# Converting a weight piece in two parts, moving three loads to another queue, and narrowing what the operand sums wait for

## The chip, the cores and the metric

The kernel runs on one core of one Trainium2 chip. The metric is the device time of one execution in microseconds (us), median of the runs. Engines are named as the profile names them: PE (TensorE matmul), PEld (its weight loads), DVE (VectorE), ACT (ScalarE), POOL (GpSimd), SP (SyncE, which here only issues DMAs; the profile calls its queue SPq).

## The reference

Two blocks follow each other. The first is a linear recurrence over time, for 4 batches, 8 heads, 768 steps and 48 channels a head:

```python
f = 1.0 / (1.0 + np.exp(-f_logit))
for t in range(S):
    state = f[:, :, t, :, None] * state + np.einsum('bhd,bhe->bhde', k[:, :, t], v[:, :, t])
    y[:, :, t] = np.einsum('bhd,bhde->bhe', q[:, :, t], state)
```

Its output is reshaped to `x`, 3072 tokens by 384 features, and goes through a multiplicative feed-forward block:

```python
a = x @ w1            # 384 x 1024
b = x @ w2            # 384 x 1024
h = a * b @ w3        # 1024 x 1024
return h @ w_out      # 1024 x 384
```

The weights arrive as 64-bit floats. A core reads them as pairs of 32-bit words and makes 32-bit floats of them.

## The kernel before

**Recurrence.** The 3072 tokens are cut into 24 chunks of 128 (`u` in the code), six to a batch. For a chunk, four loads (f, k, q, v) land; ACT turns f into gates (L523); DVE runs a forward and a backward scan over them (L531, L553) and scales q and k by the results (L547, L561). PE turns K round (L600), forms the products of K and Q inside a chunk (L576 or L586, copied by ACT at L706 or L709, masked by POOL at L715), updates the state (L632 or L692) and forms the outputs (L614 and L620, or L660 and L679, called a visit below). For chunks 0 to 4 PE turns K (L600); from chunk 5 on ACT splits K into halves of words, a DMA transposes them (L735), and ACT puts them together (L740). The outputs of chunks 0 and 1 are brought into the layout of `x` by PE (L904); those of later chunks go through DRAM, written by SP (L896) and gathered by POOL (L899).

**Weights.** `fetch` loads a piece of a weight as raw word pairs into one of a few raw areas of the tile `place`, and converts it: ACT treats the low words (L1432), DVE shifts the high words (L1447, "shift"), combines sign and low words (L1451, "sign"), and adds the two (L1457, "join"). w1 and w2 are each cut into two halves of 512 columns, so there are four pieces of 128 x 1536 numbers, called A (w1, first half), B (w2, first half), C (w1, second half) and D (w2, second half). The order `EARLY = "23ACBD"` makes DVE do the scans of chunks 2 and 3, then A, C, B and D. The raw area of A is used again by D; the raw areas that follow hold four pieces of w_out and eight of w3, in turn over three places. A load into an area waits for whatever reader `users` lists for the piece before.

**Feed-forward.** `w3 @ w_out` is formed on the core once: eight folds of 16 matmuls (L1496) need all four w_out pieces and one w3 piece each, and ACT stores their results (L1503) as `wc`. Tokens go through in six blocks of four chunks. Block 0 uses the plain product: `part` issues, for each of eight column groups `jc`, one matmul group with w1 (copied by ACT, L965) and one with w2 (multiplied on DVE, L970). Such a group is six matmul records of line L928 in 128x256 form, and is called an up group below; there are 32 of them. Later blocks use seven or fewer products on sums of the operands, so DVE forms ten sums of w1 and w2 (L1529, `w12_sums`, written over raw areas that are no longer needed) and four sums of `wc` (L1543, `wc_sums`). `down` multiplies by `wc`; its matmuls m1, m2 and m3 read `wc` itself and m4 to m7 read sums of it.

**Order of the work.** All of it is entered as tasks in `Plan`, with an engine, a cost, dependences and a priority. `listed` runs through time, always takes the task that can start first (ties go by priority), and so writes one fixed order for each engine; on the chip each engine follows its order and waits on semaphores. Where the plan leaves PE idle for at least 0.43 us in its first 130 us, matmuls on a constant are put in (`idle`, L408), so busy time of L408 is time in which PE has no work. SP's order is such a list too: a DMA that waits for its raw area holds up the DMAs behind it. In `front`, the loads of v of chunks 0 to 3 go to SP and later ones to POOL (L515).

The lines that tie the turns of DVE together are these:

```python
for a, b in zip("1" + EARLY, EARLY):
    for t in first[b]:
        t["deps"] += last[a] if a != "1" else [tk[1]["q"], tk[1]["k"]]
```

Of the kernel before, what the change touches and what calls it, by code (L numbers as in the profile page):

```python
# [37 lines left out]
I32 = mybir.dt.int32  # L38
# [7 lines left out]
P = 128  # L46
C = 128
# [35 lines left out]
WITH_DMA = 1.2  # L83
# [215 lines left out]
def ranged(ctx, tc, q, k, f_logit, v, w1, w2, w3, w_out, out, ident, w12, wc, left):  # L299
# [182 lines left out]
    def front(u):  # L482
# [30 lines left out]
        def load_v():  # L513
            s["v"] = at(12288 + NQ, DM) if u == 3 else loads.tile([P, DM], F32, name="vt")
            (nc.sync if u < UB else nc.gpsimd).dma_start(s["v"], v[u])  # L515
# [3 lines left out]
            ask[3], **({} if u < UB else {"issue": WITH_DMA, "eng": "POOL"}),  # L519
# [277 lines left out]
    def rest(u):  # L797
# [117 lines left out]
        else:  # L915
            t["z"] = moves(2, 197, 300, written, [t["y"]], n0 - 100, 0.8)
# [16 lines left out]
    def ffn(n):  # L933
# [16 lines left out]
        def part(c0, c1, jcs):  # L950
# [22 lines left out]
            for jc in jcs:  # L973
# [3 lines left out]
                pa = plan.add("PE", cost, up(jc, 0), x + pieces[0, h], n0, takes=["f"])  # L977
                ka = takes_ab(jc, plan.add("ACT", 0.2 + nt * 0.28 / 384, keep_a(jc), [pa], -10, frees=[pa]))
                pb = plan.add("PE", cost, up(jc, 1), x + pieces[1, h] + [pa], n0 - 5, takes=["f"])
# [284 lines left out]
        def down(i):  # L1264
# [99 lines left out]
            got0, got1 = (s["done"][i] + wc_sums for i in range(2))  # L1364
# [7 lines left out]
            pe("m6", m6, [q["m1"], q["S1"]], -3 if n == NB - 1 else -1, takes=["f"])  # L1372
# [3 lines left out]
            pe("m7", m7, [q["u2"], q["S2"]], -3)  # L1376
            dve("u3", 0.36, u3, [q["m7"]] + old("c22"))
            pe("m5", m5, [q["S0"], q["m2"], q["m6"]] + [q["m7"]] * (n == NB - 1), -3, takes=["f"])
            dve("c22", 0.36, c22, [q["m5"], q["u3"]] + stores[-4:-2])
            pe("m4", m4, [q["u3"]], -4)  # L1380
# [29 lines left out]
    def fetch(loads_, where, prio, due, dst, waits=(), deps=()):  # L1410
# [33 lines left out]
        s = {}  # L1444

        def shifted():
            nc.vector.tensor_scalar(m.bitcast(U32), hi, 3, None, ALU.logical_shift_left)  # L1447

        def signed():
            s["to"] = dst()  # L1450
            nc.vector.scalar_tensor_tensor(  # L1451
                s["to"].bitcast(U32), hi, 0x80000000, lo, ALU.bitwise_and, ALU.bitwise_or
            )

        def joined():
            to = s["to"].bitcast(I32)
            nc.vector.tensor_tensor(to, m.bitcast(I32), to, ALU.add)  # L1457

        past = [joins[i] for i in mine if i in joins]
        h = plan.add("DVE", 0.16 + 0.27 * w, shifted, landed + past, due, shared=True)  # L1460
        g = plan.add("DVE", 0.16 + 0.53 * w, signed, [*low, h] + list(waits), due)
        j = plan.add("DVE", 0.16 + 0.53 * w, joined, [h, g], due - 1, shared=True)
        parts.append((g, j))
        joins.update({i: j for i in mine})
        got.append(g)
        return [j]

    def weights():
        due = dict(zip(((0, 0), (1, 0), (0, 1), (1, 1)), DUE))
        for item in (x for x in EARLY if x in "ABCD"):  # L1470
# [178 lines left out]
    first, last = {}, {}  # L1649
    for item in EARLY:  # L1650
        if item in "ABCD":
            half, which = divmod("ABCD".index(item), 2)
            mine = pieces[which, half]
            first[item], last[item] = [j["deps"][0] for j in mine], mine
        else:
            t = tk[int(item)]
            first[item], last[item] = [t["p"]], [t["q"], t["k"]]
# [389 lines left out]
```

## Time and profile before

| | |
|---|---|
| Time, median of 3 runs | 452.43 us (452.41 to 453.13) |
| The profiled execution: its time, its span | 452.64 us, 450.9 us |
| PE busy | 442.3 us, 98% of the span |
| DVE busy | 357.1 us, 79% |
| ACT busy | 253.6 us, 56% |
| POOL busy | 96.0 us, 21% |
| Granted TensorE clock, mean | 0.998 |

A time in the profile counts from the start of the span. Busy PE time includes the idle-filling matmuls of L408, and the ends of matmuls are modelled, so whether PE has work is read from the chain of waits, which gives the true spacing, and from the rows of L408. The span ends 1.74 us short of the execution's time (452.64 less 450.9).

### The profile page before, as it was taken

How to read it: one execution, taken by the hardware profiler on the slowest of the kernel's cores; microseconds unless marked ns; L12 is line 12 of the kernel's file. 1: busy time of each engine (PE TensorE's matmuls, PEld its weight loads, DVE VectorE, ACT ScalarE, POOL GpSimd, SP SyncE). 2: the span in 40 equal slices, each digit the busy share in tenths (PEclk: the TensorE clock that was granted, in tenths of full speed). 3: DMA queues.
4: the chain of work that ended last, by engine and by line, in shares of the span. 5: the costliest groups of instructions: out<-in, count | busy, mean ns of one | idle time of the engine just before them, and what ended most of it. 6: DMA issues, size and time to landing. Idle time of an engine off the chain costs nothing.

```text
span 450.9 us, 11720 instructions
## 1 busy us (share of the span) xinstructions
PE 442.3 (98%) x4720; PEld 386.2 (86%) x4720; DVE 357.1 (79%) x615; ACT 253.6 (56%) x559; POOL 96.0 (21%) x132
## 2 busy tenths in 40 slices
PE   7999999999999999999999999999999999999995
PEld 6788885566899888889988889998899988889995
DVE  8999998999898978998889958965669557667541
ACT  4576245554546768676676346656666656666100
POOL 9551003133432344344333102000020000000000
PEclk9999999999999999999999999999999999999999
DMA  6998699784566786677653156563264612331111
GB/s 177 265 401 252 251 319 318 206 201 125 127 146 173 204 184 161 141 176 194 168 145 87 27 160 218 175 206 100 93 197 154 213 47 93 94 94 48 36 71 39
DMA packets 51949, 73.10 MB, mean 162 GB/s; under 512 B 22849, under 2 KB 35010, under 8 KB 50866
## 3 DMA queue, kind: packets, MB, share of 16 engines
q1 hardware_dynamic: 49202, 64.05, 48.3%
q0 software_dynamic: 2688, 8.26, 6.4%
q8 instruction: 38, 0.62, 0.6%
q14 instruction: 21, 0.17, 0.1%
HBM read 58.88 MB, written 9.04 MB: 151 GB/s over the span
## 4 chain that ended last, share of the span: by engine, by line
PE 95%; DVE 1%; SPq 1%; DMA 1%; issue 0%; POOL 0%; POOLq 0%; DVEq 0%
PE f L928 29%; PE f L1024 17%; PE l L1179 13%; PE f L1179 10%; PE f L1496 9%; PE l L928 5%; PE py L660 3%; PE pa L586 2%; PE py L679 2%; PE pa L692 2%; SPq L497 1%; PE f L408 1%; DMA ab<-in_k_dram 1%; PE l L1024 1%; DVE K L561 0%
## 5 line engine op out<-in xcount | busy, mean ns | idle before, releaser
L715 POOL TENSOR_SCALAR_AFFINE_SELECT A<-A 64x512 f32<-64x512 f32 (+1 forms) x46 | 47.7, 1037 | 45.3 <-ACT A L709 43.1
L928 PE MATMUL f<-place 128*128 128x192 f32 x240 | 42.4, 327 | 0.0
L928 PE MATMUL f<-xt,w 128*128 128x256 f32 x192 | 42.3, 380 | 0.0
L1496 PE MATMUL f<-place 128*128 128x384 f32 x128 | 42.2, 489 | 0.0
L928 PEld LDWEIGHTS f<-xt,w 128*128 128x128 f32 x192 | 36.2, 190 | 4.9
L928 PEld LDWEIGHTS f<-place 128*128 128x128 f32 x240 | 39.6, 190 | 0.2
L1024 PE MATMUL f<-xt,w 128*128 128x256 f32 x156 | 39.2, 379 | 0.0
L1496 PEld LDWEIGHTS f<-place 128*128 128x128 f32 x128 | 24.1, 190 | 16.1
L899 POOL DMA_DIRECT2D xt<-yt x22 | 16.8, 765 | 96.9 <-PE l L1179 52.3
L1024 PEld LDWEIGHTS f<-xt,w 128*128 128x128 f32 x156 | 29.6, 190 | 4.0
L531 DVE TENSOR_TENSOR_SCAN fwd<-gate,floor 112x512 f32<-112x512 f32 x24 | 30.3, 1263 | 1.0 <-ACT gate L523 0.2
L553 DVE TENSOR_TENSOR_SCAN bwd<-gate,back 112x512 f32<-112x512 f32 x24 | 29.7, 1236 | 0.7
L740 ACT COPY kt<-halves 128x896 uint16<-128x896 uint16 x19 | 22.9, 1205 | 4.7 <-DMA halves<-A 4.7
L1024 PE MATMUL f<-place 128*128 128x256 f32 x92 | 24.9, 388 | 0.0
L1432 ACT ACTIVATE place<-place 128x512 f32<-128x512 uint32 (+2 forms) x24 | 21.3, 891 | 4.8 <-DMA place<-in_w_dram 2.7
L875 ACT ACTIVATE ys<-py 112x512 f32<-112x512 f32 x22 | 13.1, 596 | 19.1 <-PE py L679 19.1
L928 PE MATMUL f<-wc,ab 128*128 128x192 f32 x128 | 23.7, 329 | 0.1
L732 ACT COPY A<-K 112x1024 uint16<-112x1024 uint16 x19 | 19.8, 1042 | 3.8 <-DVE K L561 3.8
L928 PEld LDWEIGHTS f<-wc,ab 128*128 128x128 f32 x128 | 21.2, 190 | 0.7 <-PE f L408 0.5
L523 ACT ACTIVATE gate<-f 112x512 f32<-112x512 f32 x22 | 13.9, 633 | 12.6 <-DMA f<-in_f_logit_dram 7.8
L838 POOL TENSOR_TENSOR G<-lasts,gate 112x4 f32<-112x4 f32 x20 | 9.6, 479 | 52.3 <-ACT gate L523 26.8
L515 POOL DMA_DIRECT2D vt<-in_v_dram x20 | 11.5, 575 | 40.5 <-PE py L660 35.3
(292 smaller groups left out, 1061.8 us busy)
## 6 DMA issues: line engine op xcount, KB each, us to landing
place<-in_w_dram SPq DMA_DIRECT2D x21, 512.0 KB, 6.9
A<-in_w_dram SPq DMA_DIRECT2D x19, 512.0 KB, 3.8
place<-in_w_dram SPq DMA_DIRECT2D x8, 1024.0 KB, 6.6
q<-in_q_dram SPq DMA_DIRECT2D x46, 96.0 KB, 2.9
out_dram<-o SPq DMA_DIRECT2D x23, 192.0 KB, 2.7
k<-in_k_dram SPq DMA_DIRECT2D x44, 96.0 KB, 2.8
yt<-ys SPq DMA_DIRECT2D x44, 96.0 KB, 2.9
xt<-yt POOLq DMA_DIRECT2D x22, 192.0 KB, 4.1
```

The source lines that it names most:

```text
L523: nc.scalar.activation(gate[u % 2][:, 0:NQ], fu, AF.Sigmoid)
L531: nc.vector.tensor_tensor_scan(s["P"], gate[u % 2][:, 0:NQ], floor, 0.0, ALU.mult, ALU.max)
L553: nc.vector.tensor_tensor_scan(s["R"][:, ::-1], gate[u % 2][:, NQ:0:-1], back[:, ::-1], 0.0, ALU.mult, ALU.max)
L715: nc.gpsimd.affine_select(out=a, in_=a, pattern=pattern, compare_op=ALU.is_ge, fill=0.0, base=0, channel_multiplier=-1,)
L732: nc.scalar.copy(apart.rearrange("p (two n) -> p two n", two=2), s["K"].bitcast(U16).rearrange("p (n two) -> p two n", two=2))
L740: nc.scalar.copy(to, halves.rearrange("p (two n) -> p two n", two=2))
L899: nc.gpsimd.dma_start(block_xt()[:, :, cols], s["yt"].rearrange("(k p) c -> p k c", p=P))
L928: nc.tensor.matmul(out_, lhsT=lhs[i], rhs=rhs[i], start=start and i == 0, stop=i == len(lhs) - 1, skip_group_check=True,)
L1024: nc.tensor.matmul(q[nm][:, which * TH : which * TH + TH], lhsT=lhs[i](which), rhs=rhs[i], start=start and which == 0 and i == 0, stop=i = ...
L1179: nc.tensor.matmul(banks[g, c][:, which * TH : which * TH + TH], lhsT=lhs, rhs=x_node(a), start=first and which == 0, stop=True, skip_grou ...
L1432: nc.scalar.activation(part_.bitcast(F32), part_, AF.Copy, bias=2.0, scale=2.0**-51)
L1496: nc.tensor.matmul(w3s["p", jc], lhsT=w3s[jc][:, kc * P : kc * P + P], rhs=wos[:, kc], start=(kc == 0), stop=(kc == KF - 1),)
```

## The change

It has five parts. Piece A is converted in two parts of 256 columns a row block (`CUT`, `cuts`), A0 and A1, each with its own shift, sign and join; up groups wait for the part that they read. The v loads of chunks 0, 1 and 2 are issued by ACT's queue (`BY_ACT`). The ten sums of w1 and w2 wait for the converted pieces and for the raw areas that they overwrite, instead of for the last three converted pieces of all; m1, m2, m3 and the operand sums of `down` wait for `wc`, and only m4 to m7 also for its sums. Chunk 5 is turned on PE like chunks 0 to 4. Two of the plan's estimates move (the issue of a DMA by POOL 1.2 to 1.0, the way of y through DRAM 0.8 to 2.5), the raw areas of w_out and w3 are taken one place earlier in their turn, and an area is given free by the join instead of by the sign step.

```diff
-WITH_DMA = 1.2
+CUT = "A"
+TURNS = ('2', '3', 'A0', 'A1', 'C', 'B', 'D')
+BY_ACT = (0, 1, 2)
+WITH_DMA = 1.0
...
-            (nc.sync if u < UB else nc.gpsimd).dma_start(s["v"], v[u])
+            (nc.scalar if u in BY_ACT else nc.sync if u < UB else nc.gpsimd).dma_start(s["v"], v[u])
...
-            ask[3], **({} if u < UB else {"issue": WITH_DMA, "eng": "POOL"}),
+            ask[3], **({"eng": "ACT"} if u in BY_ACT else {} if u < UB else {"issue": WITH_DMA, "eng": "POOL"}),
...
-        if u > 4:
+        if u > 5:
             crossing(u)
...
-            t["z"] = moves(2, 197, 300, written, [t["y"]], n0 - 100, 0.8)
+            t["z"] = moves(2, 197, 300, written, [t["y"]], n0 - 100, 2.5)
...
-                pa = plan.add("PE", cost, up(jc, 0), x + pieces[0, h], n0, takes=["f"])
+                pa = plan.add("PE", cost, up(jc, 0), x + pieces[0, h][: jc % KH * len(pieces[0, h]) // KH + 1], n0, takes=["f"])
...
-            got0, got1 = (s["done"][i] + wc_sums for i in range(2))
+            got0, got1 = (s["done"][i] + folds for i in range(2))
...
-            pe("m6", m6, [q["m1"], q["S1"]], -3 if n == NB - 1 else -1, takes=["f"])
+            pe("m6", m6, [q["m1"], q["S1"]] + wc_sums, -3 if n == NB - 1 else -1, takes=["f"])
...
-        h = plan.add("DVE", 0.16 + 0.27 * w, shifted, landed + past, due, shared=True)
-        g = plan.add("DVE", 0.16 + 0.53 * w, signed, [*low, h] + list(waits), due)
-        j = plan.add("DVE", 0.16 + 0.53 * w, joined, [h, g], due - 1, shared=True)
-        parts.append((g, j))
+        past = [joins[i] for i in mine if i in joins]
+        ended = []
+        for c in range(cuts):
+            def of(t, c=c):
+                t = t.rearrange("p (k n) -> p k n", k=len(loads_))
+                return t[:, :, c * t.shape[2] // cuts : (c + 1) * t.shape[2] // cuts] if cuts > 1 else t
...
+            at_once = due + 0.1 * c
+            h = plan.add("DVE", 0.16 + 0.27 * w / cuts, shifted, landed + past, at_once, shared=True)
+            g = low if by_act else [plan.add("DVE", 0.16 + 0.53 * w / cuts, signed, [*low, h, *waits], at_once)]
+            j = plan.add("DVE", 0.16 + 0.53 * w / cuts, joined, [h, *g, *waits], at_once - 1, shared=True)
+            parts.append((h, j))
+            ended.append(j)
         joins.update({i: j for i in mine})
-        got.append(g)
-        return [j]
+        got += ended
+        return ended
...
+                cuts=2 if item in CUT else 1,
...
-                [(0, 2 * DM, src)], 2048 * ((13 + i // 2) % NRAW), 25 + 2.2 * i, 45 + 2.2 * i,
+                [(0, 2 * DM, src)], 2048 * ((12 + i // 2) % NRAW), 25 + 2.2 * i, 45 + 2.2 * i,
...
-                [(0, KF * P, src)], 2048 * ((17 + jc) % NRAW), 36 + 6 * jc, 50 + 6 * jc, w3_piece(jc),
+                [(0, KF * P, src)], 2048 * ((16 + jc) % NRAW), 36 + 6 * jc, 50 + 6 * jc, w3_piece(jc),
...
-        ready = [x for p in parts[-NRAW:] for x in p] + [x for p in pieces.values() for x in p]
+        whole = [x for p in pieces.values() for x in p]
         for which in range(2):
             for i in range(5):
-                w12_sums.append(plan.add("DVE", 0.69, sum_up(i, which), ready + w12_sums[-1:], 100 + i))
+                over_ = holders((which * 5 + i) * KH * P, KH * P)
+                w12_sums.append(plan.add("DVE", 0.69, sum_up(i, which), whole + over_ + w12_sums[-1:], 100 + i))
...
-    for a, b in zip("1" + EARLY, EARLY):
-        for t in first[b]:
-            t["deps"] += last[a] if a != "1" else [tk[1]["q"], tk[1]["k"]]
+    for (_, before), (t, _) in zip(chain, chain[1:]):
+        t["deps"] += before
```

The two other m lines of `down` that read sums (m7 and m5) and m4 get `wc_sums` in the same way as m6, and the up groups with w2 are narrowed like those with w1. `by_act` is false everywhere.

More of the change, by code (lines that the diff above doesn't have):

```diff
@@ L976, in part @@
                 n0 = 100 * n + 50 + 10 * (jc >= KH)
-                pa = plan.add("PE", cost, up(jc, 0), x + pieces[0, h], n0, takes=["f"])
+                pa = plan.add("PE", cost, up(jc, 0), x + pieces[0, h][: jc % KH * len(pieces[0, h]) // KH + 1], n0, takes=["f"])
                 ka = takes_ab(jc, plan.add("ACT", 0.2 + nt * 0.28 / 384, keep_a(jc), [pa], -10, frees=[pa]))
-                pb = plan.add("PE", cost, up(jc, 1), x + pieces[1, h] + [pa], n0 - 5, takes=["f"])
+                pb = plan.add("PE", cost, up(jc, 1), x + pieces[1, h][: jc % KH * len(pieces[1, h]) // KH + 1] + [pa], n0 - 5, takes=["f"])
                 kb = plan.add("DVE", 0.16 + nt * 0.4 / 384, times(jc), [pb, ka], -10, frees=[pb])
@@ L1443, in fetch @@
         mine = range(a0 // 512, (a0 + total + 511) // 512)
[L1444 to L1457, printed above, removed]
@@ L1648, in ranged @@
             ffn(u // UB)
[L1649 to L1654, printed above, removed]
+    chain = [(tk[1]["p"], [tk[1]["q"], tk[1]["k"]])]
+    for item in TURNS:
+        if item[0] in "ABCD":
+            half, which = divmod("ABCD".index(item[0]), 2)
+            js = pieces[which, half] if len(item) == 1 else [pieces[which, half][int(item[1])]]
+            chain.append((js[0]["deps"][0], js))
         else:
             t = tk[int(item)]
-            first[item], last[item] = [t["p"]], [t["q"], t["k"]]
-    for a, b in zip("1" + EARLY, EARLY):
-        for t in first[b]:
-            t["deps"] += last[a] if a != "1" else [tk[1]["q"], tk[1]["k"]]
+            chain.append((t["p"], [t["q"], t["k"]]))
+    for (_, before), (t, _) in zip(chain, chain[1:]):
+        t["deps"] += before
     ready_at = 0.0
```

18 lines of the change are left out of this document (14 added, 4 removed).

## The prediction

> **What bounds the kernel now.** I read the page for the shares, then the busy time by stage, then the rows of line L408 alone (matmuls on a constant: PE without work), and the chain of waits last, since only it gives the true spacing of matmuls. Columns of the stage rows: stretch, its length, busy time of PE, PEld, DVE, ACT and POOL with instructions, granted clock, DMA share, GB/s.
>
> ```profile
> 35.60:61.70 26.10, 26.10 (x126) 22.96 (x123) 23.90 (x31) 12.36 (x26) 1.94 (x4) 1.00 0.81 255
> 67.10:114.00 46.90, 46.90 (x441) 28.64 (x444) 44.30 (x56) 24.02 (x44) 13.91 (x13) 1.00 0.73 209
> 122.80:446.00 323.20, 323.10 (x3536) 296.06 (x3536) 244.25 (x467) 189.53 (x433) 55.41 (x76) 1.00 0.47 134
> ```
>
> PE has no hole from 35.60 us on, at full clock; in the last stretch 0.1 us of 323.2 is missing. DVE is next: 23.90 of 26.10 us and 44.30 of 46.90 us in the stages where weights are converted, so it has little room there. Where PE only seems busy, L408 tells (columns: stretch, its length, busy time of PE and of PEld in that line, clock, DMA):
>
> ```profile
> 10.00:20.00 10.00, 3.56 (x14) 2.50 (x14) 1.00 0.89 230
> 20.00:30.00 10.00, 2.23 (x10) 1.74 (x10) 1.00 1.03 399
> ```
>
> So spare PE time lies in the first 30 us, 3.56 and 2.23 us of it in these two stretches. The chain of waits (start, length, what; a record is one pass, and an up group is six of L928) places it:
>
> ```profile
> 25.06 1.73 PE f L408 x8
> 26.79 0.44 PE py L660 x12
> ...
> 28.72 0.46 issue
> ...
> 29.73 0.63 PE f L408 x2
> 30.36 3.89 PE f L928 x18
> ...
> 61.73 0.39 PE f L600 x4
> 62.11 5.20 PE f L928 x24
> 67.31 5.16 PE f L1496 x16
> ...
> 115.59 6.67 PE f L928 x30
> 122.26 0.45 PE f L408 x2
> ...
> 122.76 1.57 PE f L928 x8
> ...
> 444.96 1.31 PE f L928 x8
> ```
>
> The first up group starts at 30.36 us. From there to 446.27 (444.96 + 1.31) PE does real work but for 0.45 us at 122.26. An up group takes 3.89 / 3 = 1.30 us, and 5.20 / 24 = 0.217 us a record is the same pitch, so nothing hides in these pieces. The reader is to see that an edit can pay only by getting up groups in ahead of 30.36, by closing the 0.45 us, or by taking work off PE. Taking waits off DVE, ACT or SP elsewhere moves nothing by itself.
>
> **Piece A in two parts.** DVE's instructions at that place (start, length, line and operation; in brackets idle time before them):
>
> ```profile
> 22.92 0.68 DVE L547 TENSOR_TENSOR Q<-place,fwd 112x512 f32<-112x512 f32 x1
> 24.22 1.28 DVE L1447 TENSOR_SCALAR place<-place 128x1536 uint32<-128x1536 uint32 x1 [0.61 <-DMA place<-in_w_dram]
> 25.42 0.34 DVE L788 TENSOR_TENSOR A<-pa,S 112x192 f32<-112x192 f32 x1
> ...
> 26.07 1.75 DVE L1451 SCALAR_TENSOR_TENSOR w<-place 128x1536 uint32<-128x1536 uint32 x1
> 27.86 1.76 DVE L1457 CUSTOM_DVE_ANT_0 w<-place,w 128x3072 uint16<-128x3072 uint16 x1
> 29.96 0.96 DVE L1447 TENSOR_SCALAR place<-place 128x1536 uint32<-128x1536 uint32 x1 [0.34 <-DMA place<-in_w_dram]
> ...
> 49.52 0.55 DVE L1447 TENSOR_SCALAR place<-place 128x768 uint32<-128x768 uint32 x1
> ...
> 50.45 0.95 DVE L1451 SCALAR_TENSOR_TENSOR place<-place 128x768 uint32<-128x768 uint32 x1
> 51.43 0.96 DVE L1457 CUSTOM_DVE_ANT_0 place<-place 128x1536 uint16<-128x1536 uint16 x1
> ```
>
> A is whole at 27.86 + 1.76 = 29.62 us, and 0.74 us later PE begins (part of that is PE's own filler). The w_out rows have exactly half of A's size: 0.55 + 0.95 + 0.96 = 2.46 us against 0.96 + 1.75 + 1.76 = 4.47, so two halves cost 4.92 us, 0.45 more. The first half begins at about 23.6 if the raw data is there (the Q row ends then), and shift, two state sums (0.34 each by their row), sign and join add to 3.2 us, with 0.3 for the slowing that the 1.28 us shift shows beside 0.96: A0 is whole near 27.1, A1 near 29.5. The halves are strided; no row shows that, and I take the packed durations, with a bound of a quarter more (1.28 / 0.96 is the nearest slowing), 1.2 us on A.
>
> When A0 is there, PE is in the visit and the products of chunk 3 (26.79 to 29.73). Then the 0.63 us of filler can hold an up group: **-0.63 us**. The 0.46 us of issue lies inside one task, whose order no edit changes: 0, at best -0.46. The 1.73 us at 25.06 lies before A0: 0, at best some of it if the whole start moves. Later pieces begin 0.6 us sooner for PE and meet DVE that gained 0.61 + 0.34 of DMA wait and lost 0.45, so C and B keep pace.
>
> **v by ACT's queue.** Rows of SP's queue, of ACT, and of DVE's scan of chunk 1:
>
> ```profile
> 5.90 0.42 SPq L515 DMA_DIRECT2D vt<-in_v_dram  x1
> 7.30 0.42 SPq L515 DMA_DIRECT2D vt<-in_v_dram  x1
> 7.83 0.84 SPq L497 DMA_DIRECT2D ab<-in_f_logit_dram  x2
> 10.57 0.43 SPq L515 DMA_DIRECT2D vt<-in_v_dram  x1
> ```
> ```profile
> 4.05 0.63 ACT L523 ACTIVATE gate<-f 112x512 f32<-112x512 f32 x1 [1.66 <-DMA f<-in_f_logit_dram]
> 7.00 0.63 ACT L523 ACTIVATE gate<-f 112x512 f32<-112x512 f32 x1 [0.83 <-DMA f<-in_f_logit_dram]
> ```
> ```profile
> 8.91 1.23 DVE L531 TENSOR_TENSOR_SCAN fwd<-gate,floor 112x512 f32<-112x512 f32 x1
> ```
>
> A v load and its step take SP 7.83 - 7.30 = 0.53 us, so loads behind all three, A's first among them, are issued 3 x 0.53 = 1.6 us sooner. That covers the 0.61 us for which DVE waits for A, which the first part counted. On ACT three issues at 0.42 to 0.53 us are 1.3 to 1.6 us, and they fit into the 1.66 us before the first gate. ACT issues no DMA in this trace; the rows of SP bound it from below, and nothing queued behind it is late unless an issue costs over 0.55 us. Against it stands that three loads of 128 x 384 numbers (197 KB each) are now asked for before k, q and f of the next chunks: at the 230 GB/s of the row of 10 to 20 us, up to 2.6 us of transfer. The second gate waits for its f until 7.00 and ends at 7.63; the scan that reads it starts at 8.91, 1.3 us later, so the loss is bounded by 2.6 - 1.3 = 1.3 us on the whole start. I take 0, since data would have to be served wholly in front of f.
>
> The Trainium skill, DMA: Bandwidth & Descriptors, section Issuing engines are not separate DMA queues, speaks against this edit: loads started by ScalarE or SyncE run on the same DMA engines and interleave, and a second issuer saves only issue time. By it the 1.6 us of issue are the whole gain and the data of f and v share the engines, which makes the loss of up to 1.3 us possible, and the sum would go from -0.69 to at worst +0.6 us. Whether two issuers share the rate can't be seen in this trace, where SP alone issues in that stretch.
>
> **Chunk 5 turned on PE.** The row at 61.73 is the same work for chunk 4: **+0.39 us** on PE, in a stage without holes. Two ACT copies and a transposing DMA go, none of which PE waited for: 0, bounds 0 and -0.39 (if it drops into a hole).
>
> **Narrower waits of the sums.** At 122.26 PE idles until the last product of block 0 is made, and the visit that could stand there is late, as these rows show:
>
> ```profile
> 111.37 0.68 DVE L1529 TENSOR_TENSOR place<-w 128x512 f32<-128x512 f32 x1
> ...
> 118.43 1.40 DVE L1543 TENSOR_TENSOR place<-wc,place 128x768 f32<-128x768 f32 x1
> ...
> 121.38 0.68 DVE L547 TENSOR_TENSOR Q<-q,fwd 112x512 f32<-112x512 f32 x1
> ```
>
> Its Q comes behind ten sums of w and four of wc. If the ten leave this place for earlier gaps, and m1 and m2 wait for no sum of wc, PE has a choice there: **-0.45 us**, bounds 0 and -0.45. I take the gain, as the Q row follows the sums directly.
>
> **Raw areas freed by the join, one place earlier in their turn.** D waits for A1 (29.5) where it waited for A's sign step (26.07 + 1.75 = 27.82), and w_out pieces wait for D's join instead of its sign step. PE has 30 records of L928 left after the folds (115.59), so it can do up groups while w_out is late, if the order says so. 0, price below. The changed estimates of the plan cost nothing; they reorder POOL and SP.
>
> **Sum.** -0.63 + 0.39 - 0.45 = -0.69 us: span 450.9 to 450.2, and with the 1.74 us around the span 451.95 for an execution like the profiled one. That one, 452.64, is 0.21 above the median, so against 452.43 the forecast is **451.74 us**, a little faster. No change is what lies within 0.2% (0.90 us): 451.53 to 453.33.
>
> **Rivals.** First, more of the start is filled: sooner raw data and A0 let PE's order hide the 0.46 us issue gap too and drop the transposes into a hole: -0.63 - 0.46 - 0.45 = -1.54, 450.9 us; with all of the 1.73 us, 449.2. For it: 3.56 and 2.23 us of L408 in 10 to 30 us. Against: DVE has no time to finish A0 before 27. Second, the gain is given back: up groups that begin 0.6 us sooner ask for D sooner.
>
> ```profile
> 41.25 1.76 DVE L1451 SCALAR_TENSOR_TENSOR w<-place 128x1536 uint32<-128x1536 uint32 x1 [0.43 <-ACT place L1432]
> ...
> 45.27 1.75 DVE L1457 CUSTOM_DVE_ANT_0 w<-place,w 128x3072 uint16<-128x3072 uint16 x1
> ```
>
> D is whole at 47.02; after 30.36 come twelve up groups (15.6 us) and a visit (from 34.25, where the first three groups end, to the dense stretch from 35.60), so PE needs it at 47.3, in the change at 46.7. The wait takes the gain, the hole at 122 stays and the transposes cost 0.39: 452.4 to 452.8 us, so the change does not do what it says. Third, slower: the w_out pieces.
>
> ```profile
> 39.94 3.99 SPq L1428 DMA_DIRECT2D place<-in_w_out_dram  x3
> ...
> 65.25 0.96 DVE L1457 CUSTOM_DVE_ANT_0 place<-place 128x1536 uint16<-128x1536 uint16 x1
> ```
>
> The third of these issues ends at 43.93, just behind D's sign step (43.01); after the change it can't go before D's join, 47.02, 4.0 us later. The last w_out join ends at 66.21, 1.1 us before the first fold at 67.31. If all the delay reaches it and the written order puts no up group in between, PE waits 4.0 - 1.1 = 2.9 us: 451.74 + 2.9 = 454.6; with one group in between (1.30), 453.3. It decides from a last join later than about 67 us.
>
> **How the numbers follow.** Forecast 0.38 (own range 451.2 to 452.4; a third of it faster, the rest no change), more filled 0.27 (faster), given back 0.17 (no change), w_out late 0.18 (slower). Faster 0.13 + 0.27 = 0.40, same 0.25 + 0.17 = 0.42, slower 0.18. The range leaves out the far end of the first rival and half of the third: 450.3 to 453.4.
>
> **What would show it.** In the profile after: the first L928 row starts near 29.7, with no filler just before it; A's shift shows no DMA wait and two short rows of each step; the second gate still ends before DVE is through with chunk 0 (if not, v's place in the queues cost time); an L600 row more among the folds; no L408 near 122; the first L1496 row within 0.5 us of an unbroken chain. The prediction is wrong if the chain shows PE waiting for DVE between 40 and 120 us, or if the stretch from the first down matmul to the end is not 323.5 us long.

## The result and the profile after

| | before | after |
|---|---|---|
| Time, median of 5 runs each, taken together | 452.77 us (452.41 to 453.23) | 456.97 us (455.69 to 458.07) |
| The profiled execution: its time, its span | 452.64, 450.9 us | 456.58, 454.8 us |
| PE busy, share of the span | 442.3 us, 98% | 442.8 us, 97% |
| DVE busy | 357.1 us, 79% | 359.1 us, 79% |

The ratio is 1.0095, with a 95% interval of 1.0082 to 1.0108: 4.2 us slower. The prediction was 451.74 us with a range up to 453.4, and slower had a chance of 0.18.

Lines after the change have other numbers: the filler is L411 (was L408), up groups and the down products of block 0 L931 (was L928), the gate L526 (was L523), the join L1467 (was L1457), folds L1508 (was L1496). First the chain of waits of the changed kernel (start, length, what):

```profile
1.57 4.32 DMA f<-in_f_logit_dram
5.98 0.64 ACT gate L526
6.64 1.24 DVE fwd L534
...
27.54 1.31 PE f L411 x6
...
30.23 1.51 PE f L931 x6
...
31.76 0.97 DVE w L1467
...
36.42 1.76 DVE w L1467
...
38.22 15.81 PE f L931 x72
...
119.98 4.10 PE f L931 x18
...
124.65 1.13 PE f L411 x4
125.78 3.90 PE f L931 x24
...
191.88 0.58 ACT a L1068
...
445.07 5.21 PE l L931 x32
```

In the kernel before, the dense stretch of up groups has this row in the chain:

```profile
35.63 4.51 PE f L928 x20
```

It begins at 38.22 instead of 35.63. Ahead of it PE has now done 24 records of up groups (6 + 18) where there were 18, as PE's rows show (start, length, line, tile; in brackets idle time before):

```profile
30.16 1.56 PE L931 MATMUL f<-xt,w 128*128 128x256 f32 x6
31.65 0.69 PE L589 MATMUL pa<-Q,K 48*64 48x64 f32 x32
32.17 0.54 PE L695 MATMUL pa<-place,kt 64*48 64x48 f32 x32
32.64 4.15 PE L931 MATMUL f<-xt,w 128*128 128x256 f32 x18
...
38.22 1.13 PE L931 MATMUL f<-xt,w 128*128 128x256 f32 x4
...
124.65 1.13 PE L411 MATMUL f<-floor 112*128 112x256 f32 x4 [0.59 <-DVE ab L973]
```

Between the first up group and 38.22 the chain runs over DVE: the join of A1 at 31.76, then all of C (w1, second half), whose join ends at 36.42 + 1.76 = 38.18. The up groups of the dense stretch start at once behind it. In the kernel before, this part of the chain is PE's.

With 0.217 us a record, the difference of 4.01 us between the ends of PE's work (445.07 + 5.21 = 450.28 against 446.27) divides without a remainder:

| Where | Working | us |
|---|---|---|
| Up to the dense stretch | 38.22 - 35.63 - 6 x 0.217 | +1.29 |
| From there to the end of the last up group | 124.08 - 38.22 - (122.26 - 35.63) + 6 x 0.217; 0.39 of it chunk 5 on PE | +0.53 |
| From the last up group to the first down product | (125.78 - 124.08) - (122.76 - 122.26) | +1.20 |
| From the first down product to the end | (450.28 - 125.78) - (446.27 - 122.76) | +0.99 |

So three stages lose about a microsecond each. The waits of PE by what ended them (total, times, longest, us) show one in each. The first row lies in the start, the last is the 0.59 above, and L1068 is the step of the chain at 191.88, which covers 0.6 of the +0.99:

```profile
PE py L603 <- DVE K L564: 2.2, 1, 2.2
...
PE f L1027 <- ACT a L1068: 0.6, 1, 0.6
PE f L411 <- DVE ab L973: 0.6, 1, 0.6
```

How the start changed is seen in the rows of ACT and of SP's queue:

```profile
0.90 1.28 ACT L421 ACT_TABLE_LOAD   x1 [0.90 <-PEq L2046]
0.96 1.34 ACTq L518 DMA_DIRECT2D vt<-in_v_dram  x3
2.19 0.20 ACT L421 ACTIVATE warm<-const-float32-0.0 112x1 f32<-112x1 f32 x1
5.98 0.63 ACT L526 ACTIVATE gate<-f 112x512 f32<-112x512 f32 x1 [3.58 <-DMA f<-in_f_logit_dram]
```
```profile
3.11 1.62 SPq L500 DMA_DIRECT2D q<-in_q_dram  x2
5.97 0.78 SPq L500 DMA_DIRECT2D f<-in_f_logit_dram  x2
```

ACT's queue issues the three v loads from 0.96 us on, while the engine is still in its table load. They compete with f of chunk 0, issued at the same time (the first experiment tests this). The first gate runs at 5.98 instead of 4.05, and SP's issue of f for chunk 1 moves from 4.04 to 5.97, the moment at which f of chunk 0 is there.

Piece A went as the edit says. DVE's rows of A, in two parts:

```profile
25.20 0.95 DVE L1458 TENSOR_SCALAR place<-place 128x768 uint32<-128x768 uint32 x1
...
27.10 0.95 DVE L1464 SCALAR_TENSOR_TENSOR w<-place 128x768 uint32<-128x768 uint32 x1
28.08 1.29 DVE L1467 CUSTOM_DVE_ANT_0 w<-w,place 128x1536 uint16<-128x1536 uint16 x1
29.30 0.94 DVE L1458 TENSOR_SCALAR place<-place 128x768 uint32<-128x768 uint32 x1
30.16 0.94 DVE L1464 SCALAR_TENSOR_TENSOR w<-place 128x768 uint32<-128x768 uint32 x1
31.76 0.96 DVE L1467 CUSTOM_DVE_ANT_0 w<-w,place 128x1536 uint16<-128x1536 uint16 x1 [0.66 <-PE f L931]
```

No shift waits for a DMA any more. But A0's shift begins at 25.20, 1.6 us later than the prediction had it, and A0 is whole at 29.37 instead of 27.1. The shift of a half takes 0.95 us, as long as that of the whole piece (0.96) and 0.40 more than that of a packed half (0.55 for w_out). So the two halves cost 2 x (0.95 + 0.95 + 0.96) = 5.72 us where nothing slows them, 1.25 more than one piece (4.47) and not 0.45. And A1's join waits 0.66 us for the first up group, which reads A0: in this trace the parts are not independent of each other; why is not shown.

### The profile page after: what moved, and what is told of

Same layout as the page of the kernel before. It is cut to its first block, busy times and chain, and to the rows that moved or that the text cites. A ratio compares the mean times of both kernels' runs of the same rounds, so it can differ in the third digit from the quotient of the medians.

```text
span 454.8 us, 11714 instructions
## 1 busy us (share of the span) xinstructions
PE 442.8 (97%) x4720; PEld 385.8 (85%) x4720; DVE 359.1 (79%) x618; ACT 252.7 (56%) x558; POOL 92.9 (20%) x132
## 4 chain that ended last, share of the span: by engine, by line
PE 93%; DVE 3%; DMA 1%; SPq 1%; issue 0%; ACT 0%; DVEq 0%; ACTq 0%
PE f L931 27%; PE f L1027 16%; PE l L1182 12%; PE f L1182 11%; PE f L1508 9%; PE l L931 6%; PE py L663 3%; PE pa L589 2%; PE py L682 2%; PE pa L695 2%; DMA f<-in_f_logit_dram 1%; PE l L1027 1%; PE f L411 1%; DVE K L564 1%; DVE w L1467 1%; DVE fwd L534 1%
## 5 line engine op out<-in xcount | busy, mean ns | idle before, releaser
L718 POOL TENSOR_SCALAR_AFFINE_SELECT A<-A 64x512 f32<-64x512 f32 (+1 forms) x46 | 44.3, 962 | 47.1 <-ACT A L712 44.8
L931 PE MATMUL f<-xt,w 128*128 128x256 f32 x192 | 43.0, 382 | 0.1
L1508 PE MATMUL f<-place 128*128 128x384 f32 x128 | 42.2, 488 | 0.0
L931 PEld LDWEIGHTS f<-xt,w 128*128 128x128 f32 x192 | 36.0, 190 | 5.1 <-DVE w L1467 0.2
L931 PE MATMUL f<-place 128*128 128x192 f32 x208 | 37.8, 328 | 0.0
L1508 PEld LDWEIGHTS f<-place 128*128 128x128 f32 x128 | 24.1, 190 | 16.1
L931 PEld LDWEIGHTS f<-place 128*128 128x128 f32 x208 | 34.2, 190 | 0.3
L1027 PEld LDWEIGHTS f<-xt,w 128*128 128x128 f32 x148 | 28.1, 190 | 3.8
L743 ACT COPY kt<-halves 128x896 uint16<-128x896 uint16 x18 | 21.6, 1203 | 15.5 <-DMA halves<-A 15.5
L931 PE MATMUL f<-wc,ab 128*128 128x192 f32 x160 | 29.3, 326 | 0.0
L931 PEld LDWEIGHTS f<-wc,ab 128*128 128x128 f32 x160 | 26.8, 190 | 0.4
L851 ACT ACTIVATE S<-S,G 112x48 f32<-112x48 f32 x72 | 18.2, 325 | 8.0 <-DVE S L794 5.6
L735 ACT COPY A<-K 112x1024 uint16<-112x1024 uint16 x18 | 18.7, 1041 | 2.6 <-DVE K L564 2.5
```

The lines of the kernel that those rows point to most:

```text
L718: nc.gpsimd.affine_select(out=a, in_=a, pattern=pattern, compare_op=ALU.is_ge, fill=0.0, base=0, channel_multiplier=-1,)
L735: nc.scalar.copy(apart.rearrange("p (two n) -> p two n", two=2), s["K"].bitcast(U16).rearrange("p (n two) -> p two n", two=2))
L743: nc.scalar.copy(to, halves.rearrange("p (two n) -> p two n", two=2))
L851: nc.scalar.activation(s["S"][:, hp], s["S"][:, hp], AF.Copy, scale=s["G"][:, hp : hp + 1])
L931: nc.tensor.matmul(out_, lhsT=lhs[i], rhs=rhs[i], start=start and i == 0, stop=i == len(lhs) - 1, skip_group_check=True,)
L1027: nc.tensor.matmul(q[nm][:, which * TH : which * TH + TH], lhsT=lhs[i](which), rhs=rhs[i], start=start and which == 0 and i == 0, stop=i = ...
```

## The experiments

All were timed in five rounds beside the kernel before, and ratios have 95% intervals. One thing is needed to read them: the span of single executions varies more than usual, since PE's clock sometimes halves in the start (last section). Where an experiment changes the plan, the written order of all engines changes with it; the text says where this was not so.

### The place of the v loads

Only v of chunks 0 to 2 moved, in the order of the kernel before: `before_v_first` (three loads) and `before_one_v_first` (chunk 0's only).

```diff
+    FIRST = []
...
+                    for go in FIRST:          # right behind the two f loads of chunk 0
+                        go()
...
+            if u > 2:                         # before_one_v_first: u > 0
                 (nc.sync if u < UB else nc.gpsimd).dma_start(s["v"], v[u])
...
+    for u in range(3):                        # before_one_v_first: range(1)
+        st[u]["v"] = loads.tile([P, DM], F32, name="vt")
+        FIRST.append(lambda u=u: nc.scalar.dma_start(st[u]["v"], v[u]))
```

> The kernel before with every engine's order kept, but ACT issues the v loads of chunks 0 to 2 first of all, as in the change; SP no longer issues them. Theory Start: f of chunk 0 lands near 5.9 us instead of 4.0, the first scan starts near 6.6, and the time rises by 1.3 to 1.9 us, to 454.1 to 454.7. Theory Order: the fillers of PE at 18.8 and 25.1 us take the delay up, and the time stays within 0.5 us of 452.77.

> The kernel before with every engine's order kept, but only the v load of chunk 0 is issued by ACT ahead of everything; those of chunks 1 and 2 stay with SP. Theory Start, by data in front of f: a third of the data, so f of chunk 0 lands 0.6 to 0.7 us later than before, and the time is 453.2 to 453.5. If it is the queue as such and not the amount of data, f is late by the same 1.9 us as with three.

Three loads: 454.38 us (453.20 to 456.73), ratio 1.0037 (1.0023 to 1.0051). One load: 452.86 us, ratio 1.0004 (0.9996 to 1.0013). ACT's rows of the two, the first gate of each:

```profile
6.01 0.63 ACT L528 ACTIVATE gate<-f 112x512 f32<-112x512 f32 x1 [3.62 <-DMA f<-in_f_logit_dram]
```
```profile
4.91 0.63 ACT L528 ACTIVATE gate<-f 112x512 f32<-112x512 f32 x1 [2.51 <-DMA f<-in_f_logit_dram]
```

The gate is late by 1.96 us with three loads ahead and by 0.86 with one. The first delay reaches the end (+1.7 us), as the first theory had it; of the second, 0.2 us is left in the medians, which is not clear of the noise.

Can the loads be taken out of the way of f and stay on ACT? `before_v_behind_gate` issues them behind the first gate in the order of before, `after_v_behind_gate` in the changed kernel.

```diff
+            if u in BY_ACT:
+                waiting.append(lambda: nc.scalar.dma_start(s["v"], v[u]))
...
+            while waiting:                    # right behind the first gate
+                waiting.pop(0)()
```

> The kernel before with every engine's order kept, but the v loads of chunks 0 to 2 are issued by ACT right behind the gate of chunk 0. Theory Start: no load stands in front of f of chunk 0, the first scan starts at 4.7; SP's queue is 1.6 us ahead, DVE's wait of 0.61 us for piece A goes, and the time is 451.9 to 452.8, no slower than before. A theory that a second issuing queue itself costs: 454 or more, as with the loads first.

> The changed kernel with every engine's order kept, but ACT issues the three v loads right behind the gate of chunk 0 (which waits for f of chunk 0) instead of ahead of it. Theory Start (the three v loads are transferred in front of f of chunk 0, so DVE's first scan starts at 6.64 instead of 4.71 us, and that delay is carried to the end): first scan back at 4.7, PE in step with before at 38 us or ahead of it, and the time falls by 1.3 to 1.9 us, to 455.1 to 455.7. Theory Order (the loss lies in the later stages as the new order puts them: chunk 5 on PE, later raw areas, a hole of 1.7 us before the down products and one of 0.6 us at 192 us): the first scan moves, but the time stays within 0.5 us of 456.97. If the start alone is the whole loss, it falls to 452.8 or below.

In the order of before: 453.01 us, ratio 1.0008 (0.9996 to 1.0021). The wait of A's shift for its DMA, 0.61 us before, is still 0.56. So freeing SP of three issues, by which the prediction removed that wait, brings nothing when f keeps its place. In the changed kernel: 457.42 us, ratio 1.0099 (1.0071 to 1.0127), no gain. That is the time of the second theory (within 0.5 us of 456.97), but not only for its reason: the start loses again what f gained. The chain shows how. f of chunk 0 is on time, but f of chunk 2 is fetched only behind v:

```profile
1.57 2.54 DMA f<-in_f_logit_dram
5.11 4.86 DMA vt<-in_v_dram
9.98 2.21 DMA ab<-in_f_logit_dram
```

ACT's order has the gate of chunk 2 ahead of work that PE needs, and PE stands still for 2.00 us at 13 us; its clock halves behind that.

Next, v by SP in the changed kernel: `after_v_by_sp` keeps the plan of the change and issues the loads from SP at fixed places, `after_v_by_sp_new_order` lets the plan write its order for it.

```diff
+                for i, (c, of_) in enumerate(((1, k), (1, q), (2, q))):   # after_v_by_sp
+                    if u == c and src is of_:
+                        waiting[i]()
...
-BY_ACT = (0, 1, 2)                                                        # after_v_by_sp_new_order
+BY_ACT = ()
```

> The changed kernel with every engine's order kept, but the v loads of chunks 0 to 2 stand in SP's queue at the places where they stood before. Theory Start (all that the v loads do happens ahead of the first up group: f late, PE idle for 2 us, its clock halved for some microseconds in some executions): first scan at 4.7 us, no PE hole of 2 us near 9 us, clock 1.00 throughout, and the time falls by what v first cost the kernel before, 1.7 us, to 455.0 to 455.5, with a spread under 1 us. The other 2.5 us stay as a matter of the later order. If the v loads are the whole loss: 452.8 or less. If they are none of it: 456.5 to 457.4.

> The changed kernel with v of chunks 0 to 2 on SP's queue in the places of the kernel before, the order written anew for it. If the place of v is the main cause, the 1.7 us that it cost in the order of before come back: 455.3 us against 457. If the order that the new estimates give is the main cause, 456 to 457.5, with the first up group near 30 us and the waits of block 1 still there.

The first: 458.22 us, ratio 1.0101 (1.0078 to 1.0123), which none of the forecasts has. In the order made for early v loads, PE waits 2.7 us for ACT's copy of ys, which stands behind ACT's work on A (its raw data lands at 22.84), and the clock halves. The two executions with a mean granted clock of 0.998 and 0.999 took 455.98 and 455.29 us, near the forecast of 455.0 to 455.5; the four with 0.992 to 0.995 took 458.21 to 460.02. So the median shows the lost clock, and says little of v itself. The second: 456.52 us, ratio 1.0091 (1.0068 to 1.0113). It is the most telling run of the study, since from the first up group to the dense stretch it has the pattern of the changed kernel, record for record, without v in front of f. PE's and DVE's rows:

```profile
28.23 1.56 PE L931 MATMUL f<-xt,w 128*128 128x256 f32 x6
...
30.71 4.15 PE L931 MATMUL f<-xt,w 128*128 128x256 f32 x18
...
36.29 1.99 PE L931 MATMUL f<-xt,w 128*128 128x256 f32 x8
```
```profile
24.34 0.95 DVE L1458 TENSOR_SCALAR place<-place 128x768 uint32<-128x768 uint32 x1 [0.59 <-DMA place<-in_w_dram]
...
26.85 0.96 DVE L1467 CUSTOM_DVE_ANT_0 w<-w,place 128x1536 uint16<-128x1536 uint16 x1
```

A0 is whole at 27.81, and the dense stretch begins at 36.29 with 24 records done: 36.29 - 35.63 - 6 x 0.217 = -0.64 us against before. I put this down to the split, though other parts of the change are in this kernel too; `after_one_part` below points the same way. In the changed kernel the same three rows stand 1.93 us later each: that is what v on ACT's queue costs, and -0.64 + 1.93 is the +1.29 of the first stage. Most of the 1.93 us gained here is lost again behind the first down product: from there to the end the chain has 326.20 us (124.25 to 450.45) against 324.50 in the changed kernel. So the median hardly moves.

### The split and the filler of the start

`before_no_first_filler` takes the 0.63 us of filler at 29.73 away; `before_two_parts_no_filler` does so too and converts A in two parts on the spot, in the order of before; `after_one_part` takes the split out of the change.

```diff
-            if ready_at and n:
+            if ready_at and n and not 28.0 < t["at"] < 30.0:   # both kernels on before
...
-CUT = "A"                                                      # after_one_part
-TURNS = ('2', '3', 'A0', 'A1', 'C', 'B', 'D')
+CUT = ""
+TURNS = ('2', '3', 'A', 'C', 'B', 'D')
```

> The kernel before, every order kept, without the two records of idle-filling matmuls (0.63 us) right ahead of the first up group. Piece A is whole at 29.62 us and PE is through with chunk 3 at 29.73, so the first up group should start at about 29.75. Theory Carried (PE has work from there to the end, so each part of a microsecond is carried): 452.0 to 452.2 against 452.7. If something behind takes the gain back: 452.7 within 0.2.

> As the kernel before without the filler ahead of the first up group, and piece A converted in two parts in the same place of DVE's order (two shifts, then sign and join of the first part, then of the second); all else as before. Theory of the prediction (the parts let PE start as soon as it is free, but PE is busy until 29.7 anyway): the same time as without the filler alone, within 0.2 us, first up group at 29.73. If the added DVE time of about 0.45 us is carried: 0.3 to 0.5 us more.

> The changed kernel with piece A in one part, the order written anew. By the theory that the split neither gains nor costs more than its 0.45 us of DVE: 456.5 to 457.5 us, with the first up group near 31 us. If the split is the cause of the loss: 455 or less.

Without the filler: 452.28 us, ratio 0.9997 (0.9987 to 1.0007); without it and with two parts: 453.00, ratio 1.0007 (0.9998 to 1.0016). By the ratios the two parts cost 0.45 us here, but the intervals overlap. The first up group starts earlier in both (29.96 and 29.51), the dense stretch hardly: 35.46 and 35.45 against 35.63. In the second kernel A1 is whole at 30.29, and the up groups come up against that:

```profile
29.51 4.55 PE L928 MATMUL f<-xt,w 128*128 128x256 f32 x18
```

18 records take 4.55 us there, where 4.05 is the length of the same row before. So A0 alone has no use when the next up groups follow directly; it pays when the order puts the products of chunk 3 in between, as the changed kernel does (L589 and L695 at 31.65 above). `after_one_part`: 457.55 us, ratio 1.0100 (1.0087 to 1.0114); the split is not the cause of the loss. In its trace the first up group starts at 32.13 us, not near 31, and with the same 24 records done the dense stretch begins at 38.89 against 38.22 in the changed kernel: 0.67 us for the split, though up to 0.32 of it can be a wait for POOL that PE has at 29.64 in the new order.

### The estimates of the plan

`before_new_estimates` changes the two estimates in the kernel before and nothing else, `before_estimate_0_9` one by 0.1, `after_old_estimates` takes both out of the change.

```diff
-WITH_DMA = 1.2
+WITH_DMA = 1.0                                                        # before_new_estimates
...
-            t["z"] = moves(2, 197, 300, written, [t["y"]], n0 - 100, 0.8)
+            t["z"] = moves(2, 197, 300, written, [t["y"]], n0 - 100, 2.5)   # before_estimate_0_9: 0.9
```

> The kernel before with nothing but the two changed estimates of the plan (POOL's issue 1.0 and y's way through DRAM 2.5): no work is added or taken away, but the whole order is written anew. Theory Order (any new order brings its own holes on PE, and the order before is one of few without): PE holes behind 115 us grow by 1 us or more and the time is 453.5 to 455. Theory Start: the start is as before, and the time is 452.3 to 453.1.

> The kernel before with one estimate of the plan moved by a tenth of a microsecond (y's way through DRAM 0.8 to 0.9). No work changes, and no engine's order changes in the first 80 us of the plan; behind that about a hundred tasks of PE and 170 of DVE stand elsewhere. Theory Order (any newly written order opens PE holes that the order before happens not to have): same start, and 453.3 to 455. If the order matters little: 452.7 within 0.3.

> The changed kernel with the two estimates of the plan as before (POOL's issue 1.2, y's way 0.8); its order is written anew. Theory Order: neither set of estimates is at fault, other holes come: 455 to 459. If the new estimates are what costs the changed kernel its time: 452.5 to 454.5.

Results: 456.77 us, ratio 1.0087 (1.0066 to 1.0109); 453.77, ratio 1.0024 (1.0015 to 1.0034); 457.14, ratio 1.0099 (1.0084 to 1.0115). Two numbers that no instruction carries make the old kernel as slow as the whole change. PE's longest wait in `before_new_estimates` lies in block 1 (the profiled execution, 459.76 us, is the slowest of its six):

```profile
PE f L1024 <- ACT a L1065: 2.5, 1, 2.5
```

Taking the estimates out of the change doesn't help either: they suffice for a loss of this size in the kernel before, and are not necessary for it in the changed one.

### Narrower waits, and chunk 5 on PE

`before_narrow_waits` has the narrower waits of the sums of w1, w2 and wc alone, `before_chunk_5_on_pe` the other turning of chunk 5 alone, and `after_chunk_5_by_dma` takes that out of the change.

```diff
-        ready = [x for p in parts[-NRAW:] for x in p] + [x for p in pieces.values() for x in p]
+        whole = [x for p in pieces.values() for x in p]                # before_narrow_waits, with the lines of m4 to m7
+                over_ = holders((which * 5 + i) * KH * P, KH * P)
...
-        if u > 4:
+        if u > 5:                                                      # before_chunk_5_on_pe; back to 4 in after_chunk_5_by_dma
             crossing(u)
```

> The kernel before with the narrower waits alone (sums of w1 and w2, sums of wc), its order written anew. By the prediction's step the hole of 0.45 us ahead of the first down product closes: 452.3 us against 452.7. By the rival theory, that what fills or opens this hole is the order written from the plan and not the waits, the hole moves to another place or grows, and the time lies between 452.5 and 454.

> The kernel before with chunk 5 turned on PE alone, its order written anew. By the prediction's step 0.39 us of PE more and nothing else: 453.1 us against 452.7. By the rival theory (any new order can open waits in block 1) 453.5 to 456.

> The changed kernel with chunk 5 turned by ACT and a DMA as before, all other parts of the change left in, the order written anew. Chunk 5 on PE, alone in the kernel before, cost 3.7 us. If it is the main cause here too, what remains is the place of v: 454 to 455 us, and the 0.6 us wait of PE near 192 us is gone. If the estimates alone are enough, as they were in the kernel before, 456 to 457.5.

Narrower waits alone: 452.89 us, ratio 1.0008 (0.9988 to 1.0028). The hole is where it was, as the chain shows:

```profile
115.90 6.67 PE f L928 x30
122.57 0.45 PE f L408 x2
```

Chunk 5 on PE alone: 456.57 us over nine executions (454.39 to 461.38), 455.87 without the slowest, ratio 1.0077 (1.0047 to 1.0108), which is 3.5 us and nearly as slow as the whole change, though its start is that of before (first fold at 67.15, before 67.14). `after_chunk_5_by_dma`: 458.10 us, ratio 1.0104 (1.0082 to 1.0126); like the estimates, this part is sufficient and not necessary. Its profiled execution lost PE's clock in the start (last section); from the first up group to the last matmul it takes 452.25 - 32.41 = 419.84 us, 0.28 less than the changed kernel (450.28 - 30.16 = 420.12). PE's row ahead of the first down product in `before_chunk_5_on_pe`:

```profile
123.27 1.13 PE L408 MATMUL f<-floor 112*128 112x256 f32 x4 [0.59 <-DVE ab L970]
124.23 1.47 PE L928 MATMUL f<-wc,ab 128*128 128x192 f32 x8
```

This is the hole of the changed kernel, to the hundredth: 0.59 of wait and 1.13 of filler. The new order makes room there and puts four filler matmuls into it, and these wait for the last product of block 0 on DVE.

### The late filler

Filler is put in only up to 100 us, which takes away the piece ahead of the first down product, in three kernels: `before_no_late_filler`, `after_v_by_sp_no_late_filler` (on top of `after_v_by_sp`) and `before_chunk_5_on_pe_no_late_filler`.

```diff
-FULL = 130.0
+FULL = 100.0
```

> The kernel before without the idle-filling matmuls after 100 us of the plan: the two records at 122.26 us go, the orders stay. Theory Filler: 0.45 us less, 452.2. If it only fills a wait: 452.66 within 0.2 us.

> As the changed kernel with v in SP's queue, and PE's idle-filling matmuls are left out after 100 us of the plan, so the four records of filler (1.13 us) ahead of the down products of block 0 go; nothing else in any order changes. Theory Filler (these records wait for the product on DVE, as the down products do, and run behind it): 1.1 us less than with v in SP's queue alone, 453.9 to 454.4. If the filler only fills a wait, the time is the same within 0.3 us.

> The kernel before with chunk 5 turned on PE, and filling only in the first 100 us, so that no matmul on a constant stands ahead of the first down product. There PE waited 0.6 us for the last product on DVE and then did 1.13 us of filler. If the filler waits for a buffer that the last product frees and so delays the down products, the stretch from the last up group to the first down product falls from 1.9 to about 0.9 us: 455.5 to 456 us against 456.6. If the down products wait for something else that ends as late, nothing changes.

In the kernel before: 452.59 us, ratio 1.0001 (0.9991 to 1.0012): its two filler matmuls stood in a wait and cost nothing that the medians show. With chunk 5 on PE: 453.70 us, ratio 1.0018 (1.0000 to 1.0035), against 456.57 with the filler; the two intervals don't overlap. PE's rows:

```profile
118.72 4.05 PE L928 MATMUL f<-xt,w 128*128 128x256 f32 x18
122.61 1.46 PE L928 MATMUL f<-wc,ab 128*128 128x192 f32 x8
```

The down products follow the up groups with no wait at all: the 1.7 us were the filler's own doing. The expectation had a stretch of 0.9 us left, and nothing is. By the names of the tiles, the filler waited for the product that reads a buffer `f`, into one of which it writes itself; the first down product waited for nothing. Behind them the chain is also 0.8 us shorter than with the filler (from its first row of L1024 to the end of the last matmul 447.73 - 143.84 = 303.89 us, against 450.17 - 145.47 = 304.70), which I can't explain from a row. In `after_v_by_sp_no_late_filler` (454.53 us, ratio 1.0058, 1.0035 to 1.0082) the same stretch shrinks by 1.7 us too, but 0.74 comes back as a wait of the down products for a sum. It is 3.7 us below `after_v_by_sp` in the median, where 1.1 was forecast, but not by the filler alone: its profiled execution kept PE's clock (mean 1.000) and the other's did not (0.992). None of the kernels beats the one before clear of the noise.

## Why the prediction was wrong

**Bound.** PE is the bound, and an edit pays only where PE has no work: right in the main. Of the 4.01 us, the rows show waits of PE in the start, ahead of the down products and in block 1, 1.13 us of filler and 0.39 of work; 0.4 of block 1 and 0.14 of the second stage I did not place. But the bound changes hands once: from 31.74 to 38.18 us the chain is DVE's, a stretch where the prediction had C keeping pace.

**Piece A in two parts.** The price on DVE was too low: sign and join of a strided half take 0.95 and 0.96 us like packed ones (the join 1.29 once), but the shift takes 0.95 instead of 0.55, and two halves 5.72 instead of 4.92 us. That lies inside the bound of 1.2 us (whose "quarter more" is a third, by 1.28 / 0.96). The gain was forecast at -0.63 us, and `after_v_by_sp_new_order` shows -0.64, `after_one_part` against the change -0.35 to -0.67. That the size came out so well is in part luck, since the reason given was half right. It is not that an up group fits into the filler's place; A1 is late then, and the split alone brings nothing in the old order. It pays because the order moves chunk 3's products behind the first up group.

**v by ACT's queue: the first step that failed.** "I take 0", since three issues fit into the 1.66 us before the first gate and a loss needs data "served wholly in front of f". The step looked at the second gate's slack, and at ACT as if its queue began with the engine's free time. ACT's queue issued at 0.96 us, during the table load, so v was loaded beside f of chunk 0, which has no slack: gate 1.93 us late, and +1.93 at the dense stretch. The bound of +1.3 was taken from the wrong chunk, and so was the sign to look for: the second gate does end (9.37) before DVE is through with chunk 0 (10.75). The Trainium skill, DMA: Bandwidth & Descriptors, section Issuing engines are not separate DMA queues, had the rule, that loads from two issuers interleave on the same DMA engines; the trace agrees, with f landing after 4.32 us against 2.54 where no v load is ahead of it.

**A's DMA wait.** The shift doesn't wait, as forecast, but because DVE came late, not because SP was free: with v on ACT behind the gate, 0.56 of the 0.61 us remain.

**Chunk 5 on PE.** +0.39 us of work came as forecast (four L603 records among the folds, 0.39 us at 82.77). What the prediction didn't count is the order that goes with it: alone, this part costs 3.5 us, and 1.7 us pass in it with the filler and its wait ahead of the down products.

**Narrower waits: -0.45 us, the second step that failed.** Alone they close nothing. In the change the hole grew from 0.50 to 1.70 us. The prediction took filler for free time that a task could use, and didn't ask what the filler itself waits for.

**"The changed estimates of the plan cost nothing": the third.** Alone they cost 4.0 us. Every part of the change rewrites the order of five engines for 450 us, and the stages behind 120 us, which the prediction held constant (323.5 us from the first down product to the end, measured 324.5), have waits that one order hides and the next doesn't.

**The rivals.** That the w_out pieces come late did not happen: no wait of PE for a fold's input is among its long ones, and the last w_out join ends at 66.38 us (66.21 before). The slower side was foreseen with 0.18, by another mechanism. The price of v was foreseen as a bound of +1.3; with it the sum was +0.6, 453.0 us, still inside the range, and it got no rival and no chance of its own.

**What stays open.** Three parts (v first, the estimates, chunk 5 on PE) cost 1.7, 4.0 and 3.5 us alone and 4.2 together, and taking any one out of the change gives back 0.5 us or nothing. I take the order that is written anew each time as the reason; that is argued, not shown. So the table of stages tells where the 4.01 us are, and the runs show -0.64, +1.93, +0.39 and, on top of `after_v_by_sp`, 1.7 us for the filler with 0.74 coming back. For the +0.99 us in block 1 I have a wait of 0.6 us (ACT's L1068), not the part of the change that makes it. The changed kernel without the late filler alone, and the raw areas' part alone, were not run.

## What to carry to other kernels

A load that is moved to an idle queue starts at once, ahead of what the first engine needs most: ask what it will share the DMA engines with, and keep it behind the first input of the critical chain. Where a planner writes the order, an edit of any cost or dependence is an edit of the whole order; cost it at the spread that such edits show (here 0 to 4 us), not at the sum of its parts. Filler matmuls are work with dependences of their own: check in PE's rows whether they run in a wait or make one.

## What the runs showed of the hardware

PE's clock halved in some executions after PE had been idle for about 2 us in the start, and stayed there for 6 to 8 us. PE's busy time in stretches of 2 us in `before_v_first` (length, busy time with instructions, granted clock, DMA share, GB/s), where PE had waited for 1.92 us up to 10.44:

```profile
9.00:11.00 2.00, 0.56 (x4) 0.88 0.80 216
11.00:13.00 2.00, 2.00 (x19) 0.50 0.75 209
13.00:15.00 2.00, 2.00 (x22) 0.50 0.79 210
15.00:17.00 2.00, 2.00 (x6) 0.50 0.86 223
17.00:19.00 2.00, 2.00 (x21) 0.92 0.88 213
```

The changed kernel's profiled execution had a wait of 2.23 us at the same place and kept its clock; `after_chunk_5_by_dma`, with 2.03 us, lost it, and its first up group starts 2.25 us later than in the change. So in these traces a wait of this length is a lottery, and it explains some of the spread of the kernels with v in front (3.5 us in `before_v_first`, whose two longest executions have the lowest mean clock, 0.992; the kernel before waits 0.73 us there and kept its clock). The spread of `before_chunk_5_on_pe`, 7.0 us, it explains in part at most: the two longest executions, 460.86 and 461.38 us, have a mean clock of 0.993 and 0.995, but the others, at 0.997 to 1.000, still spread over 3.1 us. The Trainium skill, TensorE: Matmul & The Clock Gate, section Part 1: The HAM clock gate, names an idle window of some 3.4 us, free-running against the kernel, and half clock after it. The lottery and the 0.50 agree; the length doesn't, as 2 us were enough here.
